# Attention, gated network and top-1 experts on one core: the second sweep of the gated network in two of two units, weight conversions spread over the sweeps, and the float32 form of units 3 and 4 made during the attention

## The chip, the core and the metric

The kernel runs on one core of a Trainium2 chip. A core has TensorE (PE; PEld is its weight load), VectorE (DVE), ScalarE (ACT), GpSimd (POOL), a SyncE queue (SP) that issues DMAs, and 16 DMA engines. The metric is the device time of one execution in microseconds (us), the median of several runs.

## The reference

Three networks follow each other. Lengths are 2 batches of 768 tokens (1536 rows), 512 model columns, 8 heads, 1536 hidden columns of the gated network, and 8 experts of 1024.

```python
def _moe_ref(x, w_gate, w_val, w_out, rms_g):          # the gated network
    rms = np.sqrt(np.mean(x * x, axis=-1, keepdims=True) + 1e-06)
    xn = x / rms * rms_g
    g = xn @ w_gate
    silu = g * (1.0 / (1.0 + np.exp(-g)))
    val = xn @ w_val
    return (silu * val @ w_out).astype(np.float32)

def reference(**kwargs):
    ...
    attn_out = _attn_ref(**attn_kwargs)                # local window and global columns
    x = np.ascontiguousarray(attn_out.transpose(0, 2, 1, 3)).reshape(B * S, H * D)
    x = _moe_ref(x=x, **moe_kwargs)
    return _moe2_ref(x=x, **moe2_kwargs)               # each row goes to one of 8 experts
```

The weights of the gated network arrive as 64-bit floats; attention and expert inputs are 32-bit.

## The kernel before, in words

The rows are cut into six stages of 256 rows. The attention works stage by stage in 48 small steps, and when a stage's rows are complete they are normalised and turned, in a high and a low part (`xn`).

The gated network's hidden columns are cut into 12 units of 128 columns. A unit needs three weight pieces: gate and value (`gv`) and output (`ow`). For one stage and one unit, `moe_block` makes 24 products of 128x256 (`pg`, L766), a tanh on ACT (`th`, L774), two operations on DVE (`th` L775, `hf` L779), a high part on ACT (`hid`, L783) and a low part on POOL (L784). After the units of a block it makes two output products `po` (L803, 128x512, three matmuls for each unit). `out_sum` puts the result away: in sweep 0 ACT copies it (L810), in later sweeps DVE adds it to the rows `part` (L812). The products `pg` and `po` share five PSUM banks, so a bank comes free only when DVE or ACT has read it.

There are three sweeps over the stages: sweep 0 with units 0 to 2 (partly between the attention's steps), sweep 1 with units 3 to 6, sweep 2 with units 7 to 11. After sweep 2 each stage is routed to experts (`jk`, L836, on DVE), and eight experts follow. The routing weights `rgb` are copied by ACT (L1217, four copies) between sweeps 1 and 2, into slots that units 5 and 6 leave.

A weight piece is converted from 64 to 32 bits and split (`convert64`): SP loads `raw` (L321, three slots), ACT takes the absolute value (L333), DVE does four operations (L336, L339, L342, L345) in a tile `cv` (two slots), ACT copies the high part into `gv` or `ow` (L352), POOL subtracts for the low part (L353). Units 3 to 6, 10 and 11 go to four slots in a pool `ea`, which takes the place of the attention's buffers when these are given up; units 0 to 2 and 7 to 9 go to three slots in `wp`.

Order on each engine is set by a scheduler that follows program order and its own estimate of when inputs are ready. Program order for the weights before the change is: units 0 to 2 by a table of attention steps (`PREPS`), one step at each `yield` of what is left of sweep 0 for units 3 to 6, then one step at each `yield` of sweep 1 for units 7 and 8, and units 9, 10 and 11 after it:

```python
        nx += prep_steps(PM[2], wp, 3)
        drain(f() for f in nx)
        nx = prep_steps(PM[3], wp, 3)
        for st in range(NSTAGE):
            run(moe_block(1, range(M0[st], M1), st, mpool, False))
        drain(f() for f in nx)
        nx = prep_steps(PM[4], wp, 3) + prep_steps(PM[5], ea, 4)
        drain(f() for f in nx)
```

## Time and profile before

| what | value |
|---|---|
| median of 3 runs | 680.8 us (679.8 to 686.08) |
| the profiled execution | 683.75 us |
| its span, first to last instruction | 682.1 us |
| mean granted TensorE clock | 0.984 of 2.4 GHz |
| PE busy | 635.9 us (93%) |
| DVE busy | 434.5 us (64%) |
| ACT busy | 318.2 us (47%) |
| POOL busy | 333.0 us (49%) |

PE is busy nearly everywhere, but matmuls are pipelined and busy time counts a matmul that waits in the pipeline, so the columns that PE gets through in a stretch say more than its busy share. A column is one column of a matmul's moving operand: `pg` has 256, `po` 512.

### The profile page before, as it was taken

The page shows a single profiled execution, that of the slowest core. Times are in us where ns is not written, and L with a number is a line of the kernel's source. Part 1 is how long each engine was busy: PE and PEld are TensorE (multiplying, and loading weights), DVE is VectorE, ACT ScalarE, POOL GpSimd, SP SyncE. Part 2 cuts the span into 40 slices and gives each one's busy share as a digit, 9 for nine tenths or more (in the row PEclk, how much of TensorE's full clock was granted, in tenths as well). Part 3 has the DMA queues.
Part 4 walks back from the last instruction along what each step waited for, and adds up shares of the span by engine and source line. Part 5 has one row for each costly group of instructions (what it writes and reads, how often), then busy time and mean ns, then how long its engine had stood idle before and what let it go on. Part 6 is the DMA issues. An engine that isn't in the chain of part 4 may idle for free. (4 is left out here: it accounts for less than half of the span.)

```text
span 682.1 us, 11949 instructions
## 1 busy us (share of the span) xinstructions
PE 635.9 (93%) x4280; PEld 564.0 (83%) x4281; DVE 434.5 (64%) x1191; ACT 318.2 (47%) x620; POOL 333.0 (49%) x358
## 2 busy tenths in 40 slices
PE   9998897999998799999899999899989899999992
PEld 4677787999987689999799999797788798898891
DVE  5864999965799994226469999853365454545410
ACT  3666897775554542114622221242465545555420
POOL 4435767572546643114232433451877668567501
PEclk9999999999999899999999999899989999999997
DMA  7536476620144431001421010311677677657200
GB/s 233 137 113 189 120 203 166 181 75 25 43 144 131 148 124 62 1 1 62 161 87 62 4 62 32 109 63 64 216 222 238 213 232 203 207 178 234 81 12 28
DMA packets 56569, 82.99 MB, mean 122 GB/s; under 512 B 7983, under 2 KB 38703, under 8 KB 56496
## 3 DMA queue, kind: packets, MB, share of 16 engines
q1 hardware_dynamic: 53552, 74.75, 36.5%
q0 software_dynamic: 2944, 7.35, 3.1%
q8 instruction: 37, 0.61, 0.4%
q14 instruction: 36, 0.29, 0.2%
HBM read 75.75 MB, written 7.39 MB: 122 GB/s over the span
## 5 line engine op out<-in xcount | busy, mean ns | idle before, releaser
L766 PE MATMUL pg<-xn,gv 128*128 128x256 f32 x1728 | 224.3, 284 | 7.6 <-DVE th L775 5.2
L766 PEld LDWEIGHTS pg<-xn,gv 128*128 128x128 f32 x1728 | 215.5, 192 | 13.9 <-DVE th L775 6.2
L953 POOL TENSOR_TENSOR ew<-rawe,ew 128x512 fp32r<-128x512 f32 x64 | 100.6, 1584 | 46.6 <-ACT ew L947 46.1
L803 PE MATMUL po<-ow,hid 128*128 128x512 f32 x432 | 110.9, 398 | 6.2 <-DVE th L775 3.7
L784 POOL TENSOR_TENSOR hid<-hf,hid 128x256 fp32r<-128x256 f32 x72 | 60.3, 843 | 108.8 <-ACT hid L783 106.9
L950 DVE TENSOR_TENSOR ew<-rawe,ew 128x512 fp32r<-128x512 f32 x64 | 64.0, 1004 | 72.1 <-ACT ew L947 71.3
L947 ACT ACTIVATE ew<-rawe 128x1024 fp32r<-128x1024 f32 x64 | 66.7, 1061 | 65.8 <-DMA rawe<-in_moe_w_dram 52.1
L803 PEld LDWEIGHTS po<-ow,hid 128*128 128x128 f32 x432 | 77.6, 189 | 22.0 <-DVE th L775 5.0
L1007 PE MATMUL py<-ew,eh 128*128 128x512 f32 x384 | 91.5, 396 | 1.2 <-DVE eh L1038 0.7
L1029 PE MATMUL ph<-xs,ew 128*128 128x256 f32 x672 | 85.0, 286 | 2.2 <-ACT yo L1013 1.7
L1007 PEld LDWEIGHTS py<-ew,eh 128*128 128x128 f32 x384 | 71.6, 189 | 17.9 <-DVE eh L1074 1.0
L1029 PEld LDWEIGHTS ph<-xs,ew 128*128 128x128 f32 x672 | 83.0, 193 | 3.4 <-ACT yo L1013 1.9
L783 ACT ACTIVATE hid<-hf 128x256 fp32r<-128x256 f32 x72 | 29.8, 415 | 82.8 <-DVE hf L779 82.5
L836 DVE CUSTOM_DVE_ANT_0 jk<-part,rgb 128x256 bf16<-128x256 f32 x128 | 59.5, 507 | 0.0
L558 ACT ACTIVATE pr<-pr,mx 128x256 f32<-128x256 f32 (+1 forms) x96 | 45.1, 485 | 13.6 <-DVE mx L554 12.7
L353 POOL TENSOR_TENSOR gv<-cv,gv 128x512 fp32r<-128x512 f32 x24 | 33.4, 1396 | 36.8 <-ACT gv L352 36.5
L775 DVE SCALAR_TENSOR_TENSOR th<-th,pg 128x256 f32<-128x256 f32 x72 | 29.5, 413 | 29.8 <-ACT th L774 29.8
L774 ACT ACTIVATE th<-pg 128x256 f32<-128x256 f32 x72 | 26.7, 377 | 45.8 <-PE pg L766 44.3
L342 DVE SCALAR_TENSOR_TENSOR cv<-raw,cv 128x512 uint32<-128x512 uint32 x36 | 44.2, 1227 | 0.7
L779 DVE SCALAR_TENSOR_TENSOR hf<-th,pg 128x256 f32<-128x256 f32 x72 | 29.7, 414 | 9.9 <-PE pg L766 9.1
L569 PE MATMUL pp<-ident,pr 128*128 128x128 f32 x176 | 32.1, 278 | 3.3 <-ACT ptS L577 2.2
L1038 DVE SCALAR_TENSOR_TENSOR eh<-ph,eh 128x256 fp32r<-128x256 f32 x56 | 21.7, 418 | 19.5 <-ACT eh L1037 19.5
(175 smaller groups left out, 877.6 us busy)
## 6 DMA issues: line engine op xcount, KB each, us to landing
rawe<-in_moe_w_dram SPq DMA_DIRECT2D x64, 512.0 KB, 4.1
raw<-in_moe_w_gate_dram SPq DMA_DIRECT2D x12, 512.0 KB, 3.5
raw<-in_moe_w_val_dram SPq DMA_DIRECT2D x12, 512.0 KB, 3.6
raw<-in_moe_w_out_dram SPq DMA_DIRECT2D x12, 512.0 KB, 3.6
kn<-in_k_dram SPq DMA_DIRECT2D x28, 192.0 KB, 3.3
qn<-in_q_dram SPq DMA_DIRECT2D x36, 128.0 KB, 3.2
vn<-in_v_dram SPq DMA_DIRECT2D x16, 192.0 KB, 3.2
x1d<-part SPq DMA_DIRECT2D x12, 256.0 KB, 2.1
```

What stands on the lines that cost most here:

```text
L342: nc.vector.scalar_tensor_tensor(out=t, in0=hw, scalar=0xC0000000, in1=t, op0=ALU.bitwise_and, op1=ALU.bitwise_or)
L353: nc.gpsimd.tensor_tensor(out=lo, in0=tf, in1=hi.bitcast(F32), op=ALU.subtract)
L558: pin["act"] = nc.scalar.activation(out=pr[:, j, 0:n], in_=pr[:, j, 0:n], func=ACTF.Exp, bias=mx[:, t, j:j + 1], scale=-1.0,)
L766: nc.tensor.matmul(out=pg[:, 0:n_], lhsT=gv[:, i, a, kk, :], rhs=x[st][:, kk, :], start=(n == 0), stop=(n == 3 * KD - 1),)
L784: nc.gpsimd.tensor_tensor(out=hh[:, 1], in0=hf, in1=hh[:, 0].bitcast(F32), op=ALU.subtract)
L803: nc.tensor.matmul(out=po, lhsT=hid[mi][:, a, t * P:(t + 1) * P], rhs=ow[:, c, :], start=(mi == 0 and n == 0), stop=(mi == len(ms) - 1 and ...
L836: nc.vector.tensor_tensor_reduce(out=jk, in0=part[i0 + t][:, h * 256:(h + 1) * 256], in1=rgb[h][:, e, :], scale=1.0, scalar=0.0, op0=ALU.m ...
L947: cp = nc.scalar.activation(out=t[:, 0], in_=raw, func=ACTF.Copy)
L950: nc.vector.tensor_tensor(out=t[:, 1, 0:NDV], in0=raw[:, 0:NDV], in1=t[:, 0, 0:NDV].bitcast(F32), op=ALU.subtract)
L953: nc.gpsimd.tensor_tensor(out=t[:, 1, NDV:], in0=raw[:, NDV:], in1=t[:, 0, NDV:].bitcast(F32), op=ALU.subtract)
L1007: last_mm["py"] = nc.tensor.matmul(out=py, lhsT=hid(m, a, j), rhs=w2t[m // 2][:, c, (m % 2) * DM:(m % 2 + 1) * DM], start=(n == 0), stop=( ...
L1029: nc.tensor.matmul(out=ph[:, 0:CAP], lhsT=w1t[kk][:, a, m * P:(m + 1) * P], rhs=x[:, kk, :], start=(n == 0), stop=(n == 3 * KD - 1),)
```

## The change

Sweep 1 becomes two sweeps of two units each: units 3 and 4 for all stages, then units 5 and 6 for all stages. Each of them adds its output products to `part`, so DVE makes 24 sums there where it made 12. The conversions of units 7, 8 and 9 are issued during the first of the two, one at every fourth `yield`, those of units 10 and 11 during the second, one at every fifth, and their first ACT operation is ordered behind the latest tanh. Units 10 and 11 can be converted then because units 3 and 4 are already done with.

For units 3 and 4 the first half of the conversion (`to_f32`) runs during the attention's last steps and its result goes to DRAM by a DMA that ACT issues; after the attention SP loads it back and only the split (`halves`) remains. `cv` has three slots in place of two, and the attention's key buffer shrinks to make room. Some switches that were off are removed.

```diff
-    PM = [[0, 1, 2], [3, 4, 5, 6], [], [7, 8], [9], [10, 11]]
+    PM = [[0, 1, 2], [3, 4, 5, 6], [7, 8, 9], [10, 11]]
+    NCV, NEARLY = 3, 2
-    PREPS = [2, 4, 6, 7, 11, 12, 20, 28, 36]
+    PREPS = [2, 4, 6, 7, 11, 12, 20, 28, 36] + [39, 41, 43, 45, 46, 47]
...
+        def to_f32(raw):
+            t = rp.tile([P, 512], U32, tag="cv", bufs=NCV, name="cv")
...
+            return t.bitcast(F32)
+
+        def halves(tf, hi, lo):
+            nc.scalar.activation(out=hi, in_=tf, func=ACTF.Copy)
             nc.gpsimd.tensor_tensor(out=lo, in0=tf, in1=hi.bitcast(F32), op=ALU.subtract)
 
+        def convert64(raw, hi, lo):
+            halves(to_f32(raw), hi, lo)
...
+        def early_steps(ms):
+            def step(m, i, src, a):
+                raw = load64(src, a)
+                t = early[m, i] = dram.tile([P, 512], F32, name=f"early{m}_{i}")
+                nc.scalar.dma_start(out=t, in_=to_f32(raw))
...
+        def finish(m, i, hi, lo):
+            raw = rp.tile([P, 512], F32, tag="raw", bufs=NRAW, name="rawf")
+            nc.sync.dma_start(out=raw, in_=early[m, i])
+            halves(raw, hi, lo)
...
         preps = prep_steps(PM[0], wp, 3)
+        if is_fast:
+            preps += early_steps(PM[1][0:NEARLY])
...
-        def run(g):
+        yields = [0]
+
+        def run(g, every=1):
             for _ in g:
-                if nx:
+                yields[0] += 1
+                if nx and yields[0] % every == 0:
+                    pin["act"] = pin["th"] if every > 1 else None
                     nx.pop(0)()
+                    pin["act"] = None
...
-        nx += prep_steps(PM[2], wp, 3)
         drain(f() for f in nx)
-        nx = prep_steps(PM[3], wp, 3)
-        for st in range(NSTAGE):
-            run(moe_block(1, range(M0[st], M1), st, mpool, False))
-        drain(f() for f in nx)
-        nx = prep_steps(PM[4], wp, 3) + prep_steps(PM[5], ea, 4)
-        drain(f() for f in nx)
+        for lo, hi, ms, pool, nslot, every in ((3, 5, PM[2], wp, 3, 4), (5, M1, PM[3], ea, 4, 5)):
+            nx = prep_steps(ms, pool, nslot)
+            for st in range(NSTAGE):
+                run(moe_block(1, range(lo, hi), st, mpool, False), every)
+            drain(f() for f in nx)
```

The scheduler decides where this puts the instructions. On DVE, behind the attention, the kernel before has this piece (`cv` rows are conversions, L336, L339, L342 and L345 being the four steps of one; `th` and `hf` serve the gated network):

```order
L775 SCALAR_TENSOR_TENSOR th<-th,pg 128x256
L342 SCALAR_TENSOR_TENSOR cv<-raw,cv 128x512
L345 SCALAR_TENSOR_TENSOR cv<-raw,cv 128x512
L336 TENSOR_SCALAR cv<-cv 128x512
L339 TENSOR_SCALAR cv<-cv 128x512
L342 SCALAR_TENSOR_TENSOR cv<-raw,cv 128x512
L779 SCALAR_TENSOR_TENSOR hf<-th,pg 128x256
L345 SCALAR_TENSOR_TENSOR cv<-raw,cv 128x512
```

and the changed kernel has this one on DVE in the first half of sweep 1 (there L329, L332, L335 and L338 are the four steps, L800 and L804 are `th` and `hf`, L837 is the sum):

```order
L800 SCALAR_TENSOR_TENSOR th<-th,pg 128x256
L804 SCALAR_TENSOR_TENSOR hf<-th,pg 128x256
L837 TENSOR_TENSOR part_115<-part_115,po 128x512
L837 TENSOR_TENSOR part_116<-part_116,po 128x512
L800 SCALAR_TENSOR_TENSOR th<-th,pg 128x256
L329 TENSOR_SCALAR cv<-cv 128x512
L332 TENSOR_SCALAR cv<-cv 128x512
L335 SCALAR_TENSOR_TENSOR cv<-raw,cv 128x512
L804 SCALAR_TENSOR_TENSOR hf<-th,pg 128x256
L338 SCALAR_TENSOR_TENSOR cv<-raw,cv 128x512
```

Conversions stood one behind the other with single `th` and `hf` between them; now one conversion stands between sums and `th` and `hf` of one or two units.

On ACT, near the attention's end, the kernel before has this piece (`pr` is an exponential, `ptS` a copy of turned scores, `xn` a square sum):

```order
L577 ACTIVATE ptS<-pp 128x512
L558 ACTIVATE pr<-pr,mx 128x256
L384 ACTIVATE xn_254,ss<-part_121 128x512
L558 ACTIVATE pr<-pr,mx 128x256
L577 ACTIVATE ptS<-pp 128x512
```

and the changed kernel this one, where L326 is the absolute value of an early conversion and L359 the issue of the DMA to DRAM:

```order
L326 ACTIVATE cv<-raw 128x512
L583 ACTIVATE pr<-pr,mx 128x256
L602 ACTIVATE ptS<-pp 128x512
L835 ACTIVATE part_116<-po 128x512
L508 ACTIVATE kt<-kn 128x2x384
L520 ACTIVATE qt<-qn 128x2x256
L359 DMA early_0_2025<-cv 128x512
L583 ACTIVATE pr<-pr,mx 128x256
L326 ACTIVATE cv<-raw 128x512
L409 ACTIVATE xn_254,ss<-part_121 128x512
```

Between the attention's steps ACT now starts conversions and issues their DMAs, each DMA six to nine ACT instructions behind the conversion's first step.

## Rows read from the trace of the kernel before

**Rows 1.** The page, busy time of PE, share of the span, instructions.
```profile
PE 635.9 (93%) x4280; PEld 564.0 (83%) x4281; DVE 434.5 (64%) x1191; ACT 318.2 (47%) x620; POOL 333.0 (49%) x358
```

**Rows 2.** Windows: stretch, length, then busy (count) of PE, PEld, DVE, ACT, POOL; clock, DMA.
```profile
60.00:110.00 50.00, 44.04 (x347) 40.69 (x346) 41.23 (x135) 40.30 (x93) 34.22 (x49) 1.00 0.61 170
110.00:130.00 20.00, 15.71 (x124) 14.56 (x123) 18.61 (x41) 15.90 (x34) 13.91 (x18) 1.00 0.62 162
130.00:166.00 36.00, 36.00 (x297) 34.99 (x296) 22.71 (x85) 25.20 (x54) 18.02 (x33) 1.00 0.31 86
...
181.00:262.00 81.00, 72.26 (x482) 64.73 (x481) 77.83 (x117) 37.75 (x76) 44.10 (x35) 0.98 0.44 137
262.00:315.00 53.00, 53.00 (x396) 50.05 (x394) 15.79 (x35) 12.92 (x31) 12.26 (x16) 1.00 0.00 1
315.00:330.00 15.00, 15.00 (x107) 13.99 (x106) 12.01 (x21) 6.97 (x12) 6.38 (x7) 1.00 0.39 125
330.00:352.00 22.00, 19.09 (x131) 17.37 (x130) 7.63 (x20) 11.18 (x15) 6.70 (x7) 1.00 0.43 145
352.00:440.00 88.00, 84.96 (x599) 79.03 (x599) 86.92 (x374) 19.30 (x47) 29.35 (x31) 0.99 0.14 43
```

**Rows 3.** Windows of L766 alone (`pg`) on PE: busy us and count.
```profile
0.00:181.00 181.00, 40.74 (x276) 1.00 0.49 136
181.00:262.00 81.00, 49.10 (x380) 0.98 0.44 137
262.00:315.00 53.00, 37.50 (x324) 1.00 0.00 1
330.00:352.00 22.00, 12.62 (x101) 1.00 0.43 145
```

**Rows 4.** Windows of L803 alone (`po`) on PE: busy us and count.
```profile
0.00:181.00 181.00, 14.33 (x54) 1.00 0.49 136
181.00:262.00 81.00, 28.75 (x102) 0.98 0.44 137
262.00:315.00 53.00, 17.46 (x72) 1.00 0.00 1
330.00:352.00 22.00, 7.44 (x30) 1.00 0.43 145
```

**Rows 5.** Waits of PE in 166:262: total us, times, longest.
```profile
PE po L803 <- DVE th L775: 3.7, 3, 1.3
```

**Rows 6.** Windows of tile cv on DVE: all four conversion steps, busy us and count.
```profile
0.00:60.00 60.00, 15.03 (x24) 1.00 0.56 163
110.00:130.00 20.00, 10.03 (x12) 1.00 0.62 162
181.00:262.00 81.00, 66.61 (x80) 0.98 0.44 137
315.00:330.00 15.00, 9.78 (x14) 1.00 0.39 125
```

**Rows 7.** Windows of L342 alone on DVE: busy us and count.
```profile
0.00:60.00 60.00, 4.77 (x6) 1.00 0.56 163
181.00:262.00 81.00, 30.97 (x20) 0.98 0.44 137
```

**Rows 8.** Groups by line: busy us, mean ns of one, idle before and its releaser.
```profile
L779 DVE SCALAR_TENSOR_TENSOR hf<-th,pg 128x256 f32<-128x256 f32 x72 | 29.7, 414 | 9.9 <-PE pg L766 9.1
...
L812 DVE TENSOR_TENSOR part<-part,po 128x512 f32<-128x512 f32 x24 | 15.6, 682 | 26.6 <-PE po L803 26.5
```

**Rows 9.** Timelines of ACT and PE where sweep 2 begins: start us, us, what.
```profile
330.24 4.29 ACT L1217 ACTIVATE rgb<-rawg 128x1024 f32<-128x1024 f32 x2 [2.70 <-DMA rawg<-in_moe_w_gate_dram]
...
340.49 1.68 PE L766 MATMUL pg<-xn,gv 128*128 128x256 f32 x12 [2.17 <-DVE th L775]
```

**Rows 10.** One line on SP, a DMA of 128x512 to DRAM: issue ns min/median/max.
```profile
L814 SPq DMA_DIRECT2D x1d<-part x12: 319/326/1092, 350.4 to 466.0; - x12
```

**Rows 11.** Timeline of ACT, a conversion that starts before the attention ends.
```profile
112.55 0.67 ACT L333 ACTIVATE cv<-raw 128x512 f32<-128x512 f32 x1
```

More of the change, by code (lines that the diff above doesn't have):

```diff
@@ L88 @@
     LAG1, LAG2 = 2, 3
-    CVP = 0
     KQ = (1, 0)
@@ L93 @@
     HI, HIN = ((0, 1), (0, 0)), 4
-    HCD = 0
     PTD, PTN = (0, 0), 0
-    CPOOL = 0
     TAILSEQ = "rrxrxxr"
@@ L323, in load64 @@
             return raw.rearrange("p a b t -> p (a b) t")
-        nconv = [0]
-        def convert64(raw, hi, lo):
-            n = 512
-            t = rp.tile([P, n], U32, tag="cv", bufs=2, name="cv")
+        def to_f32(raw):
+            t = rp.tile([P, 512], U32, tag="cv", bufs=NCV, name="cv")
             hw, lw = raw[:, :, 1], raw[:, :, 0]
-            nconv[0] += 1
-            hwf = hw.bitcast(F32)
-            ab = nc.scalar.activation(out=t.bitcast(F32), in_=hwf, func=ACTF.Abs)
+            ab = nc.scalar.activation(out=t.bitcast(F32), in_=hw.bitcast(F32), func=ACTF.Abs)
             if pin["act"] is not None:
                 behind(ab, pin["act"])
-            (nc.gpsimd if nconv[0] <= CPOOL else nc.vector).tensor_scalar(
+            nc.vector.tensor_scalar(
                 out=t.bitcast(F32), in0=t.bitcast(F32), scalar1=C_LO, scalar2=C_HI, op0=ALU.max, op1=ALU.min
@@ L344, in convert64 @@
             )
-            (nc.gpsimd if CVP and pin["act"] is not None else nc.vector).scalar_tensor_tensor(
+            nc.vector.scalar_tensor_tensor(
                 out=t, in0=lw, scalar=29, in1=t, op0=ALU.logical_shift_right, op1=ALU.bitwise_or
             )
-            tf = t.bitcast(F32)
-            if nconv[0] <= HCD:
-                nc.vector.tensor_copy(hi, tf)
-            else:
-                nc.scalar.activation(out=hi, in_=tf, func=ACTF.Copy)
+            return t.bitcast(F32)
+        def halves(tf, hi, lo):
+            nc.scalar.activation(out=hi, in_=tf, func=ACTF.Copy)
             nc.gpsimd.tensor_tensor(out=lo, in0=tf, in1=hi.bitcast(F32), op=ALU.subtract)
+        def convert64(raw, hi, lo):
+            halves(to_f32(raw), hi, lo)
         weights = {}
-        pin = {"act": None, "dve": None}
+        pin = {"act": None, "dve": None, "th": None}
+        early = {}
+        def early_steps(ms):
[3 more added lines that the diff above has]
+                nc.scalar.dma_start(out=t, in_=to_f32(raw))
+            steps = []
+            for m in ms:
+                c = slice(m * P, (m + 1) * P)
+                for i, (src, a) in enumerate((
+                    (w_gate[:, c].bitcast(U32).rearrange("(k p) f -> p k f", p=P), KD),
+                    (w_val[:, c].bitcast(U32).rearrange("(k p) f -> p k f", p=P), KD),
+                    (w_out[c, :].bitcast(U32).rearrange("p (a f) -> p a f", a=1), 1),
+                )):
+                    steps.append(lambda m=m, i=i, src=src, a=a: step(m, i, src, a))
+            return steps
+        def finish(m, i, hi, lo):
+            raw = rp.tile([P, 512], F32, tag="raw", bufs=NRAW, name="rawf")
+            nc.sync.dma_start(out=raw, in_=early[m, i])
+            halves(raw, hi, lo)
         def prep_steps(ms, pool, nslot):
@@ L365, in gv @@
                     t = weights[m, 0]
+                    if (m, i) in early:
+                        finish(m, i, *(t[:, i, a].rearrange("p k f -> p (k f)") for a in range(2)))
+                        return
                     raw = load64(w[:, m * P:(m + 1) * P].bitcast(U32).rearrange("(k p) f -> p k f", p=P), KD)
@@ L370, in ow @@
                     t = weights[m, 1] = pool.tile([P, 2, DM], F32R, tag="ow", bufs=nslot, name=f"ow{m}")
+                    if (m, 2) in early:
+                        finish(m, 2, t[:, 0], t[:, 1])
+                        return
                     raw = load64(w_out[m * P:(m + 1) * P, :].bitcast(U32).rearrange("p (a f) -> p a f", a=1), 1)
@@ L434, in prep @@
                     nat = [
-                        pool.tile([P, 2 * STAGE if x == "q" else 2 * DM if x == "k" else (ST_MAX + 1) * VW], F32, tag=f"{x}n", bufs=2, name=f"{x}n") for x in "kqv"
+                        pool.tile([P, 2 * STAGE if x == "q" else 2 * (ST_MAX + 1) * P if x == "k" else (ST_MAX + 1) * VW], F32, tag=f"{x}n", bufs=2, name=f"{x}n") for x in "kqv"
                     ]
@@ L773, in moe_block @@
                 th = pool.tile([P, STAGE], F32, tag="th", bufs=2, name="th")[:, 0:n_]
-                nc.scalar.activation(out=th, in_=pss[0][:, 0:n_], func=ACTF.Tanh, scale=0.5)
+                pin["th"] = nc.scalar.activation(out=th, in_=pss[0][:, 0:n_], func=ACTF.Tanh, scale=0.5)
                 nc.vector.scalar_tensor_tensor(
@@ L1011, in second_layer @@
                         n += 1
-                yo = rp.tile([P, DM], F32, tag="cv", bufs=2, name="yo")
+                yo = rp.tile([P, DM], F32, tag="cv", bufs=NCV, name="yo")
                 nc.scalar.activation(out=yo, in_=py, func=ACTF.Copy, scale=gwl[j])
@@ L1164, in body @@
                 late_loads()
-            while preps and nun > PREPS[9 - len(preps)]:
+            while preps and nun > PREPS[len(PREPS) - len(preps)]:
                 preps.pop(0)()
```

## The prediction

> **What bounds the kernel now.** I first read the totals [rows 1]: PE is busy for 93% of the span, so a gain must come from stretches in which PE gets through fewer columns than it could. The windows by stage [rows 2] show where that is, and they have to be read with the counts of `pg` and `po` [rows 3, 4], since PE's busy time hides part of it. In 262:315, part of sweep 1 with no conversion running, PE did 324 products of 256 columns and 72 of 512, that is 119,808 columns in 53 us, or 2,260 in a us. That is my rate for PE undisturbed. In 181:262 it did 380 and 102, that is 149,504 columns, which is 66.1 us of work in 81 us: 14.9 us were lost. In 330:352 it did 101 and 30, that is 41,216 columns, 18.2 us of work: 3.8 us were lost.
>
> Who holds PE in 181:262 is in its longest wait [rows 5]: `th` on DVE. DVE is 77.83 of 81 us busy there [rows 2], and 66.61 of that are conversion steps [rows 6]: twenty conversions lie one behind the other, and the two short operations of 0.41 us [rows 8] which give PE its banks back queue among them. Directly behind it, in 262:315, DVE has 15.79 us to do in 53. The work is there at the wrong time. In 330:352 it is another engine: ACT makes two copies of `rgb` in a row, 4.29 us, after 2.70 us of waiting for their load, and PE then waits 2.17 us for a `th` that stands behind them [rows 9].
>
> **The change part by part.** *What can be won* is 14.9 + 3.8 = 18.7 us. The number of products of PE stays the same, so whatever remains is a wait.
>
> *Price of a conversion on DVE.* Four steps: 15.03 / 6 = 2.51 us at the start, 10.03 / 3 = 3.34 in 110:130, 66.61 / 20 = 3.33 in 181:262, and 9.78 / 3.5 = 2.79 in 315:330 [rows 6]. For spaced conversions beside the gated network I take 2.79, the row most like what comes; 2.51 and 3.33 are the ends.
>
> *What is left of sweep 0.* Of its 432 products `pg` and 108 `po`, 276 and 54 are done by 181 [rows 3, 4]; the other 156 and 54 are 67,584 columns, 29.9 us of PE. DVE now has six conversions there (units 5 and 6), 6 x 2.79 = 16.7 us, and 6.5 unit-stages of two operations, 6.5 x 0.83 = 5.4: 22.1 us in 29.9, or 74%. The six splits of units 3 and 4 need ACT and POOL alone. At 80% of DVE (12.01 of 15 in 315:330) PE showed no idle time [rows 2]. The scheduler has put the six close together, so I leave 1 us of loss.
>
> *First half of sweep 1.* Twelve unit-stages are 110,592 columns, 48.9 us. DVE has nine conversions, 25.1 us, twelve pairs `th` and `hf`, 12 x 0.83 = 9.9, and twelve sums, which are new, 12 x 0.68 = 8.2 [rows 8]: 43.2 us, or 88%. Rows with a fuller DVE: at 96% (181:262) PE lost 18%, at 99% in 352:440, where the operations are short, 3 of 88 us were idle [rows 2]. Between those and no loss at 80% I take 5%, 2.5 us. *Second half:* six conversions, 16.7 + 18.1 = 34.8 us in 48.9, 71%, no loss. Two blocks of two in place of one of four need 12 banks where 10 were needed, and the bank of a `po` now waits for a sum in DVE's queue; 1.5 us for that. Together 5 us, bounds 2 and 10 (at 3.33 a conversion the first half has 30.0 + 18.1 = 48.1 us on DVE, 98%, and PE would lose as in 181:262).
>
> *Where sweep 2 begins.* The copies of `rgb` stay, two of them in a row again; only the conversions of units 9 to 11 between them go. I keep 3.2 of the 3.8 us, bounds 2 and 4.
>
> *The attention's end.* This is the price. Two of the six early conversions start before the attention's end already, the first at 112.55 [rows 11], and wait there in the two `cv` slots, so four more come in there, all behind 112 us. DVE had 18.61 us in 110:130 and 22.71 in 130:166 [rows 2], 41.3 in 56; four more at 3.34 are 13.4, so 54.7 in 56. PE is 36.00 of 36 busy in 130:166 and only 15.71 of 20 in 110:130, where DVE is 93% full: that is the fullest that DVE gets in the attention. At 93% 54.7 us take 58.8, 2.8 more than now. Against that, the spacing takes one conversion out of 110:130. I take 2.0 us; bounds -1 (2.51 us each: 51.3 / 0.93 = 55.2) and 10.3 (DVE no fuller than the 82% of 60:110: 54.7 / 0.825 = 66.3).
>
> *DMAs that ACT issues.* Six, a kind of issue that ACT has nowhere in the trace before; the nearest row is SP's of the same shape, 0.33 us [rows 10], so 2.0 us of ACT, which has 10.8 us free in 130:166 [rows 2]. The ACT queue also stands at each of them until DVE has finished that conversion, and the exponentials stand behind. The scheduler puts six to nine ACT instructions between a conversion's first step and its DMA, about as long as the conversion takes. I take 0.7 us, bounds 0 and 20 (six times a whole conversion of 3.33). The loads back are SP's, six of half the size of those they replace, in a stretch where the DMA engines are less than half busy; they cost nothing as long as that holds, and six issues of 0.33, 2.0 us, if it doesn't.
>
> *The sum:* 18.7 - 5.0 - 3.2 - 2.0 - 0.7 = 7.8 us. The profiled execution took 683.75 us (span 682.1 and 1.65 around it), so 676.0 on its scale. It lies 2.95 above the median; on the median's scale it is **673.0 us**.
>
> **A rule weighed against the rows.** The step L342 takes 4.77 / 6 = 0.80 us at the start and 30.97 / 20 = 1.55 in 181:262 [rows 7], for the same shape, and POOL is 44.10 of 81 us busy in the latter [rows 2]. The Trainium skill, SBUF — State Buffer, section "SBUF: two separate sides", says that DVE and GpSimd share one pair of ports under an exclusive lock, which a DVE operation with two SBUF inputs contends for, and that the loser waits for the whole instruction. By that rule the longer steps would be waits for POOL's subtractions of the previous conversion, spaced conversions would get the short price, and the sum would come out as in rival 1. The two prices of L342 agree with it; no row shows a spaced conversion in the sweeps.
>
> **The rivals.**
> 1. *Spaced conversions are cheap.* DVE steps run beside POOL's subtractions only when conversions follow each other closely. Spaced ones cost 2.51 us as at the start [rows 6], the sweeps lose 2 us, the boundary 2, the attention gains 1: 18.7 - 2 - 2 + 1 - 0.7 = 15.0, or 665.8 us. Against it: POOL still has the low parts of `hid`, and the row of 315:330 gives 2.79.
> 2. *The first half of sweep 1 is as full as 181:262 was.* At 3.33 each, DVE's 98% holds PE again: a loss of 10 in place of 5, 678.0 us. This is also how the change would fail to do what it says, as far as pacing goes; the order on DVE speaks against that, since it shows one conversion at a time.
> 3. *The attention pays.* DVE stays at the 82% that it has in 60:110 and the attention ends 10.3 us later in place of 2.0: 18.7 - 5.0 - 3.2 - 10.3 - 0.7 = -0.5, 681.3 us.
> 4. *Slower: ACT stands at its own DMAs.* Each of the six waits for DVE's last step with the attention's exponentials behind it; DVE then waits for these, and PE for both. Fully exposed it is 20 us: 18.7 - 5.0 - 3.2 - 2.0 - 20 = -11.5, or 692.3 us. It makes the kernel slower than before from 8.5 us of exposed waits on, less than half of it. For it: in 130:166 PE has no idle time at all in which a wait could hide [rows 2]. Against it: the distance in ACT's queue.
>
> **How the numbers follow.** Forecast (668 to 677) 0.49, at 673.0; rival 1 0.16; rival 2 0.16; rival 3 0.11; rival 4 0.08. What a measurement of this kernel can tell from no change is about 1%, 6.8 us. Faster by more than that is under 674.0: six tenths of the forecast's share, 0.30, rival 1's 0.16 and 0.04 from rival 2's better end, so 0.50. Slower by more is over 687.6: most of rival 4 and a little of rival 3, 0.07. The rest, 0.43, lies between. The range reaches from rival 1 to just past rival 3: 665 to 682, which leaves out most of rival 4 and the far ends of the others.
>
> **What the profile after would show.** The rate of PE behind the attention: near 2,200 columns in a us through sweep 1 if the first term is right, near 1,850 in its first half if rival 2 is. DVE: 70 to 90% in all stages of sweep 1 in place of 96% and then 30%. The attention should end (before: by the end of 130:166) some 2 us later; 10 later is rival 3, and a line of ACT's waits at the DMA to DRAM with several us is rival 4. The mean of a conversion's four steps decides between 2.51, 2.79 and 3.33. The stall at `rgb` should still be there. What would make the prediction wrong beside these is a new stretch with a lower granted clock or a later stage, sweep 2 or the experts, that takes back what sweep 1 gives, since their work is not changed.

## The result and the profile after

The changed kernel takes 675.83 us (median of 4 runs, 673.28 to 678.7), the kernel before 682.26 us beside it (4 runs): a ratio of 0.9878, 95% interval 0.9835 to 0.992. The profiled execution took 675.75 us, 8.0 less than the one of before, where the sum had said 7.8; on the medians the gain is 6.4. Taken once more in a later comparison the change stood at 0.9876 (0.9844 to 0.9907). So it is faster by 1.2%, with an interval clear of no change, at 675.8 in place of the forecast's 673.0 us. By the prediction's own line ("faster" under 674.0 us) the median falls just into its middle band, which had a chance of 0.43; as a ratio the gain is past the 1% for which that line stood. The terms of the sum did not each come out as written. Medians here are over all executions, while ratios and intervals leave out four executions in a slow state (691.27, 712.17, 1570.08 and 3481.01 us, two of them of the kernel before).

In the tables by stage below, "exponentials" are the 96 of the attention (L558 before, L583 after; the 73rd opens their last quarter), and "first store" is the first `x1d` DMA (L814, L839), by which the first stage of sweep 2 is done. The times are those at which these instructions start in the profiled executions.

| us | start to 73rd exponential | 73rd to last exponential | last exponential to first store | first store to last stage's store | of it the last stage | rest | span |
|---|---|---|---|---|---|---|---|
| before | 121.2 | 38.6 | 190.6 | 115.0 | 25.8 | 216.7 | 682.1 |
| after | 121.3 | 45.4 | 179.6 | 111.8 | 21.6 | 216.0 | 674.1 |
| difference | 0.1 | 6.8 | -11.0 | -3.2 | -4.2 | -0.7 | -8.0 |
| after, profiled again later | 124.0 | 46.5 | 178.5 | 111.7 | 21.6 | 217.2 | 677.9 |

The last row says how far one profile can be trusted. The same kernel's last exponential starts at 166.7 us in one profile and at 170.5 in the other. Behind sweep 2 ("rest"), whose work no kernel of this document changes, the 14 profiles take from 214.8 to 219.5 us.

The totals of the profile after, against [rows 1]: no engine is busy for less time, apart from POOL's 3 us. DVE's total holds twelve more sums, so its conversions have become shorter.

```profile
PE 636.4 (94%) x4280; PEld 565.2 (84%) x4281; DVE 434.1 (64%) x1203; ACT 318.2 (47%) x620; POOL 330.0 (49%) x358
```

The windows of the profile after, cut by its own stages, with the columns of [rows 2] (busy us and count of PE, PEld, DVE, ACT and POOL, then the granted clock and DMA):

```profile
200.00:225.00 25.00, 23.33 (x154) 20.44 (x153) 19.30 (x31) 10.61 (x23) 13.79 (x12) 1.00 0.35 111
225.00:270.00 45.00, 45.00 (x328) 42.29 (x327) 33.84 (x63) 18.48 (x39) 19.85 (x20) 1.00 0.32 98
270.00:318.00 48.00, 47.46 (x342) 44.33 (x341) 31.91 (x58) 15.65 (x35) 17.39 (x17) 1.00 0.22 71
318.00:330.00 12.00, 11.55 (x85) 10.83 (x85) 3.93 (x9) 10.01 (x10) 2.21 (x3) 1.00 0.51 173
```

The same windows for `pg` alone (L791 on PE), which answer to [rows 3]:

```profile
200.00:225.00 25.00, 15.39 (x118) 1.00 0.35 111
225.00:270.00 45.00, 33.35 (x264) 1.00 0.32 98
270.00:318.00 48.00, 34.91 (x272) 1.00 0.22 71
318.00:330.00 12.00, 9.15 (x73) 1.00 0.51 173
```

and for `po` alone (L828), which answer to [rows 4]:

```profile
200.00:225.00 25.00, 10.05 (x36) 1.00 0.35 111
225.00:270.00 45.00, 17.30 (x64) 1.00 0.32 98
270.00:318.00 48.00, 19.62 (x70) 1.00 0.22 71
318.00:330.00 12.00, 3.50 (x12) 1.00 0.51 173
```

Counted as in the prediction, at 2,260 columns in a us, 225:270 holds 264 x 256 + 64 x 512 = 100,352 columns, 44.4 us of work in 45; 270:318 holds 46.7 in 48; 318:330 holds 11.0 in 12; 200:225 holds 21.5 in 25. So the two halves of sweep 1 run at 2,230 and 2,197 columns in a us, where before 181:262 (the rest of sweep 0 and the first part of sweep 1) ran at 1,846. What is left to lose is 3.5 us in the rest of sweep 0 and some 3 us behind it. DVE has 33.84 of 45 and 31.91 of 48 us to do: the hump of 96% and the valley of 30% of [rows 2] are gone.

The conversions, by windows of tile `cv` on DVE (four steps each), against [rows 6]:

```profile
0.00:60.00 60.00, 14.98 (x24) 1.00 0.57 165
130.00:168.00 38.00, 14.89 (x20) 0.91 0.49 145
200.00:225.00 25.00, 15.51 (x19) 1.00 0.35 111
225.00:270.00 45.00, 20.69 (x32) 1.00 0.32 98
270.00:318.00 48.00, 16.71 (x24) 1.00 0.22 71
```

That is 2.59 us (20.69 / 8) and 2.79 us (16.71 / 6) for a spaced conversion in the two halves of sweep 1, and 3.27 (15.51 / 4.75) in what is left of sweep 0, where they still follow each other. The step that was longest before is L342, which is L335 after (min, median and max ns, first and last start). Before:

```profile
L342 DVE SCALAR_TENSOR_TENSOR cv<-raw,cv x36: 674/1186/1756, 15.6 to 328.2; 128x512 uint32<-128x512 uint32 x36
```

After:

```profile
L335 DVE SCALAR_TENSOR_TENSOR cv<-raw,cv x36: 678/694/1754, 15.1 to 312.8; 128x512 uint32<-128x512 uint32 x36
```

The same 36 steps of the same shape have a median of 694 ns in place of 1186. This median alone does not measure the spacing, though: the kernel without spacing (below), which gains nothing, has 693.

```profile
L335 DVE SCALAR_TENSOR_TENSOR cv<-raw,cv x36: 677/693/1782, 16.1 to 291.0; 128x512 uint32<-128x512 uint32 x36
```

Which of the four steps gets long depends on the order, so all four have to be taken together. Undisturbed, two of them take 0.43 us and two 0.69. Count as long a step that takes over 1.3 times as much. Behind 170 us, 35 of 100 steps are long before and 22 of 84 after, and they take 25.0 and 12.5 us more than undisturbed ones; in the kernel without spacing it is 28 of 84 and 20.6 us. Of L342 alone, the 23 steps over 0.9 us before, and the 11 of L335 after, all overlap an instruction of POOL; the 5 and 10 that overlap none took 0.68 to 0.70 us. By the Trainium skill, SBUF — State Buffer, section "SBUF: two separate sides", such a step waits while GpSimd holds the shared ports; that long steps stand beside POOL's instructions, and nowhere else, agrees with it.

The price stands ahead of all this. The last exponentials start at 159.7 us before and at 166.7 after; the windows of the profile after around that end:

```profile
150.00:160.00 10.00, 8.11 (x61) 7.02 (x59) 9.97 (x27) 7.58 (x17) 5.99 (x7) 1.00 0.43 131
160.00:170.00 10.00, 9.81 (x48) 8.93 (x48) 4.20 (x18) 3.81 (x9) 1.82 (x6) 0.66 0.25 69
170.00:180.00 10.00, 10.00 (x81) 9.65 (x81) 4.07 (x15) 4.40 (x11) 2.12 (x3) 1.00 0.01 2
```

DVE is full (9.97 of 10), PE has gaps (8.11 of 10) where it had none in 130:166 before [rows 2], and then, with PE busy again, its clock stands at 0.66 for 10 us. Most of what PE waits for in 110:170 is DVE, the attention's maxima above all (total us, times, longest):

```profile
PE sp L572 <- DVE mx L579: 2.9, 4, 1.2
PE pg L791 <- DVE hf L804: 1.3, 1, 1.3
```

The DMAs that ACT issues are there, six of them, and cost 0.35 us of ACT each (the line on ACT's queue: ns min/median/max, first and last start):

```profile
L359 ACTq DMA_DIRECT2D early<-cv x6: 337/349/417, 124.0 to 159.0; - x6
```

No wait of ACT at one of them appears among its waits in 110:170; the longest there is 2.9 us for PE's turned scores.

Where sweep 2 begins, ACT makes the same two `rgb` copies in a row as in [rows 9] (timeline of ACT):

```profile
317.56 4.32 ACT L1247 ACTIVATE rgb<-rawg 128x1024 f32<-128x1024 f32 x2 [2.23 <-PE pg L791]
```

They no longer wait for their load, and all that PE waits for in 318:345 is one `hid`, 0.5 us.

### The profile page after: what moved, and what is told of

Its sections match the earlier page's. It is cut to its first block, busy times and chain, and to the rows that moved or that the text cites. A ratio compares the mean times of both kernels' runs of the same rounds, so it can differ in the third digit from the quotient of the medians.

```text
span 674.1 us, 11985 instructions
## 1 busy us (share of the span) xinstructions
PE 636.4 (94%) x4280; PEld 565.2 (84%) x4281; DVE 434.1 (64%) x1203; ACT 318.2 (47%) x620; POOL 330.0 (49%) x358
## 5 line engine op out<-in xcount | busy, mean ns | idle before, releaser
L791 PE MATMUL pg<-xn,gv 128*128 128x256 f32 x1728 | 227.0, 284 | 2.4 <-DVE hf L804 1.8
L791 PEld LDWEIGHTS pg<-xn,gv 128*128 128x128 f32 x1728 | 218.3, 191 | 9.6 <-DVE hf L804 2.5
L828 PE MATMUL po<-ow,hid 128*128 128x512 f32 x432 | 115.8, 399 | 2.8 <-POOL hid L809 1.0
L809 POOL TENSOR_TENSOR hid<-hf,hid 128x256 fp32r<-128x256 f32 x72 | 58.4, 814 | 109.6 <-ACT hid L808 109.4
L828 PEld LDWEIGHTS po<-ow,hid 128*128 128x128 f32 x432 | 76.2, 191 | 16.5 <-POOL hid L809 2.2
L583 ACT ACTIVATE pr<-pr,mx 128x256 f32<-128x256 f32 (+1 forms) x96 | 45.1, 483 | 20.6 <-DVE mx L579 18.9
L800 DVE SCALAR_TENSOR_TENSOR th<-th,pg 128x256 f32<-128x256 f32 x72 | 29.8, 414 | 32.7 <-ACT th L799 32.5
L345 POOL TENSOR_TENSOR gv<-cv,gv 128x512 fp32r<-128x512 f32 x20 | 27.6, 1381 | 30.7 <-ACT gv L344 30.4
L804 DVE SCALAR_TENSOR_TENSOR hf<-th,pg 128x256 f32<-128x256 f32 x72 | 29.8, 415 | 11.7 <-PE pg L791 10.2
L837 DVE TENSOR_TENSOR part<-part,po 128x512 f32<-128x512 f32 x36 | 23.4, 682 | 19.7 <-PE po L828 19.7
```

What stands on the lines that cost most here:

```text
L583: pin["act"] = nc.scalar.activation(out=pr[:, j, 0:n], in_=pr[:, j, 0:n], func=ACTF.Exp, bias=mx[:, t, j:j + 1], scale=-1.0,)
L791: nc.tensor.matmul(out=pg[:, 0:n_], lhsT=gv[:, i, a, kk, :], rhs=x[st][:, kk, :], start=(n == 0), stop=(n == 3 * KD - 1),)
L800: nc.vector.scalar_tensor_tensor(out=th, in0=th, scalar=1.0, in1=pss[0][:, 0:n_], op0=ALU.add, op1=ALU.mult)
L809: nc.gpsimd.tensor_tensor(out=hh[:, 1], in0=hf, in1=hh[:, 0].bitcast(F32), op=ALU.subtract)
L828: nc.tensor.matmul(out=po, lhsT=hid[mi][:, a, t * P:(t + 1) * P], rhs=ow[:, c, :], start=(mi == 0 and n == 0), stop=(mi == len(ms) - 1 and ...
```

## The experiments

All times are medians; each ratio is to the kernel before in the same comparison, with its 95% interval.

**Is it the early part or the sweeps?** The early part taken out, all else as in the change:

```diff
-    NCV, NEARLY = 3, 2
+    NCV, NEARLY = 3, 0
-    PREPS = [2, 4, 6, 7, 11, 12, 20, 28, 36] + [39, 41, 43, 45, 46, 47]
+    PREPS = [2, 4, 6, 7, 11, 12, 20, 28, 36]
```

> The change without its early part: units 3 and 4 are loaded and converted behind the attention as before, all else as in the change. My theory (the early conversions cost the attention some 6.7 us and save about as much behind it): the attention's last product ends near 166 us as before, DVE is full again in the rest of sweep 0 with twelve conversions, PE loses 5 to 9 us more there than in the change, and the time is within 3 us of the change, 674 to 679 us. Rival (the early part is what made the gain): 680 or more. Rival (the early part is a price and nothing else): 670 or less.

Measured: 675.23 us, 0.9871 (0.983 to 0.9913). With three `cv` slots the early part is worth nothing that can be measured. Its absence did not bring the attention's end back to the expected 166 us, though: the last exponential starts at 169.3.

The early part alone, with sweep 1 in one piece and a conversion at every `yield`, as before:

```diff
-        for lo, hi, ms, pool, nslot, every in ((3, 5, PM[2], wp, 3, 4), (5, M1, PM[3], ea, 4, 5)):
-            nx = prep_steps(ms, pool, nslot)
-            for st in range(NSTAGE):
-                run(moe_block(1, range(lo, hi), st, mpool, False), every)
-            drain(f() for f in nx)
+        nx = prep_steps([7, 8], wp, 3)
+        for st in range(NSTAGE):
+            run(moe_block(1, range(M0[st], M1), st, mpool, False))
+        drain(f() for f in nx)
+        nx = prep_steps([9], wp, 3) + prep_steps([10, 11], ea, 4)
+        drain(f() for f in nx)
```

> The early conversions of units 3 and 4 alone, with sweep 1 in one piece of four units and conversions at every yield as before. My theory (the gain is in the spacing of the conversions over sweep 1, and the early ones cost the attention what they save): about as before, 679 to 685 us; the attention ends some 5 to 7 us later, and PE still loses 8 to 10 us in a piece with DVE over 95% busy. Rival (the early part made the gain): 672 to 677.

Measured: 692.77 us, 1.0125 (1.009 to 1.0161), slower, and outside both expected ranges. The attention ends late (170.7) and nothing comes back: from there to the first store it is 189.6 us, against 190.6 before. With six conversions gone from the rest of sweep 0, those of units 7 to 9 follow at once, and the windows show the old hump in its old place, DVE 24.80 of 25:

```profile
200.00:225.00 25.00, 20.96 (x142) 18.27 (x141) 24.80 (x37) 13.01 (x27) 14.65 (x11) 1.00 0.46 147
225.00:270.00 45.00, 39.09 (x255) 34.83 (x255) 37.82 (x60) 17.44 (x38) 20.75 (x18) 0.96 0.43 129
```

**Is it the cut or the spacing?** The cut kept, the spacing taken out, and with it the order behind the tanh, which the kernel keeps only where `every` is over 1; then half of the spacing; then the spacing without the cut (units 10 and 11 must then wait until sweep 1 is over):

```diff
# no_pace: every = 1, 1
+ ((3, 5, PM[2], wp, 3, 1), (5, M1, PM[3], ea, 4, 1))
# pace_half: every = 2, 2
+ ((3, 5, PM[2], wp, 3, 2), (5, M1, PM[3], ea, 4, 2))
# one_sweep_paced: one piece, every = 6
+ ((3, M1, [7, 8, 9], wp, 3, 6),)
+        nx = prep_steps([10, 11], ea, 4)
+        drain(f() for f in nx)
```

> The change with a conversion at every yield in both halves of sweep 1, not at every fourth and fifth, and not held behind the tanh. My theory (the spacing made most of the gain): conversions of units 7 to 9 follow each other, DVE is over 95% busy for some 35 us in the first half, PE loses 5 to 7 us more than in the change: 680 to 683 us. Rival (the cut of sweep 1 in two, which lets units 10 and 11 be converted before sweep 2, made it): as the change, 674 to 677 us.

> The change with a conversion at every second yield in both halves of sweep 1 in place of every fourth and fifth. If what counts is how full DVE is, DVE has one conversion (2.8 us) for each 2.7 us of PE's work until the first half's nine are made, beside 1.2 us of other work, so it is overfull for some 30 us: half to two thirds of the loss without spacing, 678 to 682 us. Rival (any spacing that keeps the tanh ahead of a conversion is enough): as the change, 673 to 676 us.

> The change with sweep 1 in one piece again (units 3 to 6), but still spaced: units 7, 8 and 9 are converted at every sixth yield of it, behind the tanh; units 10 and 11 behind it, all at once. The early part stays. My theory (the spacing makes the gain, the cut only lets units 10 and 11 be spaced too): most of the gain stays, 676 to 680 us against 683 of before; six conversions lie close together where sweep 2 begins and PE loses 2 to 5 us there. Rival (the cut itself makes the gain): 683 or more. Rival (the cut is only a price, for its sums and banks): 672 to 675.

| every | ratio (interval) | us | last exponential | from it to the first store |
|---|---|---|---|---|
| 1 and 1 | 1.0033 (1.0005 to 1.0061) | 685.74 | 168.0 | 189.5 |
| 2 and 2 | 0.9979 (0.9951 to 1.0008) | 682.9 | 168.6 | 185.5 |
| 4 and 5 (the change) | 0.9878 (0.9835 to 0.992) | 675.83 | 166.7 | 179.6 |
| 6, one piece | 0.9895 (0.9861 to 0.993) | 677.69 | 167.8 | 181.0 |

The stretch behind the attention follows the spacing like a dose, 189.5, 185.5, 179.6 us; between the second and the third the spacing is all that differs. In this stretch the cut by itself gives nothing (189.5 against the 189.6 of the early part alone, which is uncut and unspaced), and with the spacing it adds 1.4 us, or 2.5 by the change's second profile, which the intervals of the whole do not separate. The whole tells more: without spacing the cut kernel takes 685.74 us and the uncut one 692.77, with intervals apart, though both lie outside what was expected of them (680 to 683 and 679 to 685). In the profiles 1.5 us of that lies in sweep 2's last stage (see the end of the next section), 2.7 in the attention, where both have the same order of instructions but the clock fell in the uncut one alone (0.67 in 160:170, against 1.00), and 2.3 behind sweep 2, whose cause stays open. The half-spaced kernel's 682.9 us are just past the expected 678 to 682. The windows of the kernel without spacing show the hump again, with the price of crowding: 28 steps in 22.81 us, 3.26 us a conversion (tile `cv` on DVE):

```profile
200.00:225.00 25.00, 22.81 (x28) 1.00 0.49 147
225.00:270.00 45.00, 26.86 (x36) 0.96 0.38 118
```

**Why does the attention end late?** First the DMAs in ACT's queue, the fourth rival. They are issued by SP instead:

```diff
-                nc.scalar.dma_start(out=t, in_=to_f32(raw))
+                nc.sync.dma_start(out=t, in_=to_f32(raw))
```

> The change with the six DMAs to DRAM issued by SP in place of ACT. My theory (the attention's end is late because DVE is full there): the attention ends as late as in the change, within 1.5 us, and the time is 674 to 678 us. Rival (ACT stands at its DMAs with the exponentials behind it): the attention ends 3 to 6 us earlier and the time is 669 to 673 us.

Measured: 674.91 us, 0.9881 (0.9843 to 0.9919), the same as the change. From the 73rd exponential to the last it is 42.5 us in place of 45.4. The clock of 130:168 is 1.00 here and 0.91 in the change; three other kernels with the change's order in the attention, and its DMAs on ACT, run there at 1.00 too and take 44.1 to 44.6. So about 2 us may come from the queue, and the whole doesn't show it. The rival that ACT stands at its DMAs for long is out.

Then the place of the conversions: all fifteen sooner, so that the last third gets fewer; and unit 2 sooner without the early part:

```diff
# sooner_sp (stores by SP)
+    PREPS = [2, 4, 6, 7, 11, 12, 16, 18, 20] + [23, 27, 31, 35, 39, 43]
# unit2_sooner (NEARLY = 0)
+    PREPS = [2, 4, 6, 7, 11, 12, 16, 20, 24]
```

> The change with unit 2 converted sooner and the six early conversions spread over attention steps 23 to 43 in place of 39 to 47, stores issued by SP. If DVE being full at the attention's end is what the early part costs (4 to 5 us in its last third), this takes half or more of it off: 669 to 673 us, with the last exponential at 160 to 164 us. Rival (DVE is as full in the middle of the attention, so the price only moves): 673 to 677 us, last exponential at 165 to 168. Rival (SP stands at its stores with the attention's loads behind it): 677 or more.

> The change without its early part, and with unit 2 converted sooner (attention steps 16, 20 and 24 in place of 20, 28 and 36), since without the early part PE stood 3.8 us for unit 2's output weights at 124 us and the clock fell. If that stall, and not the end of the attention as such, made the attention late there, the last exponential comes at 160 to 163 us in place of 169 and the time is 667 to 671 us, less than the change: the early part would be needless. Rival (the attention's middle has no room either): 674 to 678 us.

Measured: 678.06 us, 0.9899 (0.9863 to 0.9934), and 682.76 us, 0.9965 (0.9932 to 0.9998). The last exponential starts at 167.7 and 170.3; the delay has only moved, to ahead of the 73rd exponential (134.5 and 136.3 us from the start in place of 121.3), and behind it 33.1 and 34.0 us remain. It does not show that DVE has no room there: between 100 us and the 73rd exponential DVE is busy for 76% of the time in both kernels and PE for 94 and 95%, where before, in the same part of the attention, DVE is busy for 92% and PE for 84%. Later, PE's longest wait in 110:170 is for POOL, which had itself waited 3.0 and 3.1 us for the attention's own load of `vn` and then worked without a pause. The lines (total us, times, longest) are the first kernel's and the second's:

```profile
PE sp L572 <- POOL vn L454: 4.2, 2, 3.9
PE sp L572 <- POOL vn L454: 4.2, 1, 4.2
```

What makes these loads late was not tried, so for the first kernel the third thing expected of it, SP standing at its stores, is not excluded. The second kernel's 682.76 us lie outside both ranges expected of it; beside the kernel without the early part, 4.4 of the 6.2 us between the two profiles lie behind sweep 2.

This left the third `cv` slot, which all kernels so far had in common. With two slots and no early part the order of instructions on every compute engine is that of the kernel before until past the attention; with three it differs from the attention's middle on:

```diff
-    NCV, NEARLY = 3, 2
+    NCV, NEARLY = 2, 0      # two_slots (PREPS without the six)
+    NCV, NEARLY = 2, 2      # two_slots_early
```

> No early part, and two cv slots as before the change; spacing and the cut of sweep 1 stay. Up to the attention's end the order of instructions is then that of the kernel before on PE, DVE, ACT and POOL, while with three slots it differs from the attention's middle on. Theory (the attention ends 7 to 10 us later in every changed kernel because the third cv slot, with or without the early part, lets another conversion in between its steps and turns its order): the last exponential starts near 160 as before (159.7) in place of 166.7 to 170.3, and the spacing still takes its 10 us or so from there to the first stage of sweep 2 (some 180 to 183), so 668 to 671 us. Rival 1 (the time is given back: two slots and twelve conversions in what is left of sweep 0 make that stretch longer by what the attention gains): last exponential near 160, then 187 or more, 675 us. Rival 2 (the late end has nothing to do with the order, for instance the clock): the end stays at 167 to 170 and the time at 675.

> The change as it is, with two cv slots in place of three. Theory (early conversions lengthen the attention by themselves as the third slot does, since six conversions more on DVE in its last third): last exponential near 167 to 170 and 674 to 678 us. Rival (the third slot is the whole cause): the last exponential starts near 160 to 163, 668 to 671 us. If the first kernel of this call has its end near 160 and this one near 168, both the slot and the early part can cause the delay, each alone.

Measured: 672.28 us, 0.9822 (0.9794 to 0.985), and 673.98 us, 0.9846 (0.981 to 0.9882). The first misses its expected 668 to 671 us by one. The last quarter of the attention in the four combinations, from the 73rd exponential to the last:

| us | two slots | three slots |
|---|---|---|
| no early part | 37.8 | 46.4 |
| early part | 43.6 | 45.4 |

(38.6 before.) Profiles with the same order of instructions up to there say how sure this is. Six have that of the change (three slots, the early part, its stores on ACT): 44.1 to 47.0 us, the last exponential at 166.7 to 170.7. Three have that of the kernel before (itself, the two-slot kernel and the last version below): 37.8 to 38.6 us, the last exponential at 159.7 to 162.2. So two things lengthen the attention, each alone, and they don't add. The shrunk key buffer, which is in all changed kernels, can cost the attention no more than the 2.5 us between 159.7 and 162.2. How the third slot does it is read from the traces. With it and no early part, the timeline of PE has, in the attention's middle (start, us, what, idle before),

```profile
123.10 0.71 PE L828 MATMUL po<-ow,hid 128*128 128x512 f32 x2
128.27 1.23 PE L828 MATMUL po<-ow,hid 128*128 128x512 f32 x4 [3.79 <-POOL ow L345]
```

and with two slots

```profile
124.00 0.62 PE L828 MATMUL po<-ow,hid 128*128 128x512 f32 x2
124.66 1.70 PE L791 MATMUL pg<-xn,gv 128*128 128x256 f32 x12
126.79 1.20 PE L828 MATMUL po<-ow,hid 128*128 128x512 f32 x4
```

Three conversions are under way on DVE there in place of two, POOL's last split of unit 2's output weights starts at 126.96 in place of 125.44, and the scheduler has put no `pg` between the two pieces of `po`, so PE stands 3.79 us. Behind that the clock is 0.92 in 130:168, with two slots 1.00. The early part fills DVE: its kernel with two slots in 130:168,

```profile
130.00:168.00 38.00, 34.02 (x257) 30.94 (x256) 35.37 (x97) 26.88 (x56) 20.43 (x30) 1.00 0.51 156
```

against the same window of the kernel with two slots and no early part:

```profile
130.00:168.00 38.00, 38.00 (x313) 37.01 (x312) 24.91 (x87) 27.65 (x59) 19.77 (x34) 1.00 0.30 81
```

DVE 35.37 us for 24.91, PE 34.02 for 38.00. Of the 5.8 us that the early part takes it gives back 5.0 behind the attention, where 181.4 us become 176.4: six conversions moved from one full place to another.

**A version that follows from this.** Two slots, no early part, and the rest of sweep 0 relieved as well: unit 6 goes to the first half of sweep 1, unit 9 to the second, nine conversions in each stretch. Beside it the change once more:

```diff
-        nx = prep_steps(PM[1], ea, 4)
+        nx = prep_steps([3, 4, 5], ea, 4)
-        for lo, hi, ms, pool, nslot, every in ((3, 5, PM[2], wp, 3, 4), (5, M1, PM[3], ea, 4, 5)):
-            nx = prep_steps(ms, pool, nslot)
+        first = prep_steps([6], ea, 4) + prep_steps([7, 8], wp, 3)
+        second = prep_steps([9], wp, 3) + prep_steps([10, 11], ea, 4)
+        for lo, hi, nx, every in ((3, 5, first, 4), (5, M1, second, 4)):
```

> Two cv slots and no early part, as in the kernel with two slots, and three conversions each moved one stretch later: unit 6 from what is left of sweep 0 to the first half of sweep 1, unit 9 from the first half to the second (nine conversions in each stretch in place of twelve, nine and six). In the two-slot kernel 200:225 holds 116 products of 256 columns and 30 of 512, 45,056 columns, 19.9 us of work in 25 at 2,260 in a us: 5.1 us are lost there, DVE being 22.6 of 25 us busy. Theory (what is still lost in sweep 0's rest is DVE's fullness): three conversions less leave 1 to 2 us of that loss, and nine conversions with 18.1 us of other work fit into the 48.9 us of the second half as they do into the first: 3 us less from the attention's end to sweep 2, 669 us. Rival (the loss there is the wait for the first weights of units 3 and 4 after the attention, whatever follows them): the loss stays and the second half loses 1 to 2 us more, 672 to 674 us.

> The change itself once more, unaltered, to stand on the same chip as the kernel above and to narrow its interval: 0.984 to 0.992 of the kernel before. If the kernels with two slots are better than the change by what the attention's end shows (5 us), their ratios (0.9822 for the one without the early part) lie below this one's interval; if the ratio here is 0.983 or lower, the gain of the two slots is not shown.

Measured: 669.16 us, 0.9777 (0.9747 to 0.9807), and the change 676.6 us, 0.9876 (0.9844 to 0.9907), on the same chip. The intervals are apart: the balanced version beats the change by 1% and the kernel before by 2.2%. From the last exponential (162.2) to the first store it takes 178.2 us, 3.2 less than with two slots alone, as expected. Its windows of all engines:

```profile
200.00:225.00 25.00, 24.15 (x169) 22.20 (x168) 15.83 (x26) 10.39 (x23) 10.92 (x11) 1.00 0.28 85
225.00:270.00 45.00, 45.00 (x324) 42.05 (x323) 37.14 (x66) 17.69 (x39) 20.86 (x20) 1.00 0.32 101
270.00:318.00 48.00, 46.85 (x340) 43.66 (x339) 36.49 (x66) 23.59 (x40) 20.04 (x19) 1.00 0.36 111
```

With 133 `pg` and 36 `po` in 200:225, PE does 23.2 us of work there in place of 19.9, so 1.8 us are lost where 5.1 were; the second half pays about 1 us (277 and 63 in 270:318, 45.6 us of work in 48, where the change did 46.7). That the two-slot kernel by itself beats the change is likely, not shown: 0.985, its interval's upper end, lies inside the interval of the change's second measurement.

## Why the prediction came out

Where PE was losing time, and why, was read rightly: DVE's crowded conversions, not the work. The forecast's mechanism holds, and the three kernels with different spacing show it. By its own steps:

- *The sweeps and the start of sweep 2,* 18.7 won less 5.0 and 3.2 kept, so 10.5: measured 11.0, and 12.1 in the second profile (last exponential to first store). The parts inside were mixed. The first half of sweep 1, taken at 88% of DVE and 2.5 us of loss, had 75% and lost 0.6; the second, taken at 71% and none, had 66% and lost 1.3; the copies of `rgb`, taken at 3.2 kept, lost 1.0; the rest of sweep 0, taken at 1.0, lost 3.5 in 200:225 alone, since its conversions are not spaced.
- *Price of a conversion,* taken as 2.79: 2.59 and 2.79 in sweep 1. Rival 1's mechanism (crowding, not the work, makes conversions dear) is right; its price of 2.51 is nearly reached in the first half. Its time failed because the attention paid. The rule weighed beside it rested on the two prices of L342; that step's median turned out to be as short without spacing, and what bears the rule out is where the long steps stand.
- *The attention's end* is the term that was mis-sized: 2.0 + 0.7 taken, 6.8 measured between the 73rd exponential and the last. From the start to the last exponential it is 7.0 and 10.8 us in the change's two profiles, and 7.6 between the means of the profiles that share the one order and the other. The row taken for DVE's fullness, 93% in 110:130, was not too optimistic for DVE (9.97 of 10 in 150:160), but PE, which before had no idle time in 130:166, has gaps beside a DVE as full as that. The clock adds less: with the same order it fell at the attention's end in three profiles (0.66, 0.66 and 0.67 in 160:170; 45.4, 46.5 and 47.0 us) and stayed at 1.00 in three (44.1, 44.2 and 44.6). The third rival, the attention pays (10.3), was nearer in size than the forecast; its time failed because the sweeps gave a little more than it had kept and sweep 2 gave 3.2. The third slot was costed at nothing; alone it takes 8.6 us (46.4 less 37.8), more than the early part's 5.8.
- *ACT's DMAs,* 0.7: some 2 us at most by the experiment; the fourth rival is refuted.
- *Sweep 2,* taken as unchanged, gave 3.2 us that no term had, and this hid the attention's excess: 4.1 us too little there, 3.2 too little here. That the sum met the profiled execution to 0.2 us is luck in these two, and luck in the execution: the second profile's span is 4.2 us less than the one of before, not 8.0.

The gain in sweep 2 lies in its last stage, 25.8 us before and 21.6 after. The windows before:

```profile
433.50:439.50 6.00, 3.28 (x21) 2.59 (x19) 5.71 (x24) 1.16 (x2) 2.60 (x2) 0.94 0.36 94
439.50:445.50 6.00, 5.96 (x28) 5.96 (x29) 2.02 (x7) 2.14 (x3) 3.10 (x3) 0.50 0.46 169
```

and after:

```profile
430.50:436.50 6.00, 4.18 (x28) 3.40 (x27) 5.70 (x24) 1.44 (x3) 2.61 (x2) 1.00 0.42 94
436.50:442.50 6.00, 6.00 (x55) 6.00 (x53) 2.85 (x10) 2.68 (x5) 3.51 (x4) 1.00 0.49 169
```

DVE is as full with the routing in both; PE got 3.28 us of work in the first 6 us before and 4.18 after, and behind it the clock stands at 0.50 (1.2 GHz) before and at 1.00 after, with 28 and 55 instructions in the next 6 us. The scheduler put other products between the routing's small ones.

It is tempting to say that the new order keeps the clock up. The other profiles speak against it. The three kernels with sweep 1 in one piece have the old order in this stage, those with the cut another, nearly the same in all of them. With the old order the stage takes 25.8 us (before, clock 0.50), 24.6 (the early part alone, 0.72) and 23.1 (one piece, spaced), where the clock stays up:

```profile
432.10:438.10 6.00, 3.15 (x21) 2.46 (x20) 5.71 (x24) 1.16 (x2) 2.54 (x2) 1.00 0.34 95
438.10:444.10 6.00, 6.00 (x52) 6.00 (x53) 1.96 (x7) 2.15 (x3) 3.28 (x3) 1.00 0.50 167
```

With the new order it is 21.5 or 21.6 us in ten profiles at a clock of 1.00, and 23.1 in the kernel without spacing, whose order there is the change's and whose clock was 0.75:

```profile
447.10:453.10 6.00, 6.00 (x41) 6.00 (x41) 2.88 (x10) 2.94 (x5) 3.58 (x3) 0.75 0.45 164
```

So of the 4.2 us the order is worth 1.5 (23.1 to 21.6, both at 1.00), which comes with the cut, and the clock the other 2.7. The order does not settle the clock: it fell in two of three profiles with the old one and in one of eleven with the new one. What does settle it stays open.

## What to carry to other kernels

Work that is off the critical path still has to be spread: when a helper engine is full in one stretch and idle in the next, space its steps before cutting their cost; here giving out a conversion at every fourth or fifth `yield`, behind the tanh, in place of every one was worth 10 us, and the steps became cheaper as well. Moving such work ahead pays only if the place it goes to has room on every engine that waits there, so look for a stretch with idle time on the helper, not for the earliest one. A further buffer is not free: it lets a scheduler start work sooner, and what then comes ahead of what should be tried with the old number. One profile of a kernel is one draw: here two of the same kernel were 3.8 us apart, half of the gain to be explained.

## What the runs showed of the hardware

Gaps in PE's work can cost twice. Behind a stretch in which PE was 8.11 of 10 us busy the granted clock was 0.66 over the next 10 us, with PE busy again, and in the kernel before, behind 3.28 of 6, it was 0.50, the lower of its two levels, for 6 us. Elsewhere such a gap went free: 7.19 of 10 in 150:160 of the kernel with its stores on SP, with a single gap of 2.11 us behind it, and 34.02 of 38 in the kernel with two slots and the early part, all at 1.00.

The same instructions in the same order, with nearly the same gaps, met either level. PE's gaps of over 0.3 us in 150:168 were 1.26, 0.65, 0.32, 0.41 and 0.71 us in the early part alone, and 1.23, 0.65, 0.31, 0.41 and 0.72 without spacing:

```profile
160.00:170.00 10.00, 8.52 (x42) 7.76 (x42) 7.16 (x27) 4.06 (x9) 2.04 (x4) 0.67 0.46 143
160.00:170.00 10.00, 8.72 (x57) 7.28 (x58) 6.94 (x27) 5.79 (x12) 2.70 (x7) 1.00 0.45 131
```

In sweep 2's last stage gaps of 1.92 and 0.82 us came before a clock of 0.50, and gaps of 2.00 and 0.82 us, with one piece and spacing, before 1.00. What decides between the two, these runs don't settle.

A conversion's four steps on DVE, 128x512 in 32 bits, took 2.59 us spaced (225:270 of the change) and 3.33 crowded (181:262 before), 3.26 in the kernel without spacing, the work being the same. In none of the 14 profiles is a step long that overlaps no instruction of POOL: 55 to 73 steps in each.
